# Two subtractions of VectorE issued two steps sooner in the preparation of batch 0's heads

## The chip, the cores and the metric

The kernel runs on one NeuronCore of a Trainium2 chip, in one launch. The metric is the device time of the program in microseconds (us); less is better. Five engines work beside each other and meet at semaphores: TensorE (PE) multiplies into PSUM, VectorE (DVE), ScalarE (ACT) and GpSimd (POOL) do elementwise work, and SyncE (SP) issues DMAs. Each engine takes its own instructions strictly in the order in which they stand in its queue.

## The reference, cut to what matters

```
q, k, v: (2 batches, 8 heads, 768 tokens, 64), proj: (64, 6)
bucket(q), bucket(k) = six sign bits of q @ proj, of k @ proj
scores = q @ k.T / 8, and -1e9 where the buckets differ
x = softmax(scores) @ v
u = x + real(fft over tokens and channels of x)
u = u + relu(layernorm(u) @ w1) @ w2
y = w_tok_r @ (u cos(u @ w_theta)) + w_tok_i @ (u sin(u @ w_theta))
out = (u + y) + relu((u + y) @ w_ch)
```

## The kernel before, in words

All float32 products are done as products of a rounded high part and a low part (the value less its high part): three products, high by high, high by low, and low by high.

Batch 0's attention is the first stage (`attention_first`, L450). It takes the 8 heads as 4 pairs, j = 0 to 3, and for each pair 6 tiles of 128 queries, L = 0 to 5. One tile of one pair, both heads at once, is a step s = 6 j + L; there are 24. In each step TensorE forms the scores of two heads in two of three PSUM tiles (`pair_S`, tile `pss`), VectorE takes the negated maximum of each (TENSOR_REDUCE `nm`), ScalarE takes the two exponentials. Two in three of the exponential tiles are split into high and low by GpSimd (a TENSOR_SCALAR, then a TENSOR_TENSOR) and turned by a DMA. The third is turned by TensorE in two halves (`turn_half`, L364): three transposes into the PSUM tile `psm`, ScalarE's copy of the high part, VectorE's subtraction of the low part. The trace names these tiles by their buffers, p, pt, w1h and w1l, some of them lent from the weights. `psm` has one buffer in this stage, so the second half's transposes wait for the first half's subtraction.

In a step the program gives VectorE, in this order: pieces of the Fourier stage of an older pair (`fold`, tile `fa`), the first halves' subtraction, two maxima, the second halves' subtraction, then the normalisation of a finished pair (r, x) and the preparation of the next pair. Within the stage this order is binding: `Ordered` chains each engine's instructions one behind the other as the program gives them, SP's and GpSimd's DMA issues included. What is outside the stage, the first pair's preparation among it, is ordered by the compiler's list scheduler from priorities and a simulated timeline.

The preparation of pair j + 1 is the generator `prep_pair` (L230), advanced once in a step. Its parts, split by `yield`:

1. At L = 5 of the pair before: the loads of q and k (tile `tt`) on SP.
2. At L = 1: two copies on ScalarE, the high parts `hi` of q and of k (tile `stk`, 0.125 folded into k's).
3. At L = 2: TensorE projects q and k, VectorE makes the sign bits (TENSOR_SCALAR `bits`, from PSUM).
4. At L = 3: TensorE spreads q's bits, ScalarE makes `oh` of q, and VectorE subtracts the low part `lo` of q (SCALAR_TENSOR_TENSOR `stk<-tt,stk`, helper `stt`).
5. At L = 4: the same for k, and the load of v.
6. At L = 3 of the pair's own steps: ScalarE's and VectorE's high and low part of v (`vv`). In a step with L = 3 and j over 0 this stands ahead of part 4 of the next pair.

Both `lo` parts are read by the scores of the next pair, from its L = 0 on.

Of the kernel before, what the change touches and what calls it, by code (L numbers as in the profile page):

```python
# [16 lines left out]
ALU = mybir.AluOpType  # L17
# [16 lines left out]
def f(t):  # L34
    return t.bitcast(F32)
# [35 lines left out]
def fused_kernel(ctx, tc, A, out):  # L71
    nc = tc.nc
    V, AC, PE, PL, SY = (Ordered(tc, e) for e in (nc.vector, nc.scalar, nc.tensor, nc.gpsimd, nc.sync))
# [4 lines left out]
    def mk(p, shape, dt, tag, **kw):  # L78
        return p.tile(shape, dt, tag=tag, name=tag, **kw)

    def mm(o, l, r, st, sp):
        PE.matmul(o, l, r, start=st, stop=sp)
# [4 lines left out]
    def stt(eng, out, in0, in1, op, scale=1.0):  # L87
        if eng is V:
            return V.scalar_tensor_tensor(out=out, in0=in0, scalar=scale, in1=in1, op0=ALU.mult, op1=op)
        assert scale == 1.0  # L90
        return eng.tensor_tensor(out=out, in0=in0, in1=in1, op=op)
# [23 lines left out]
    def PS(k):  # L115
        n = turn[k] % sum(c for _, c in ring[k])
        turn[k] += 1
        for p, c in ring[k]:
            if n < c:
                w = [128, 2, 512] if k == "s" else [128, 512]  # L120
                tag = "psm" if p in [x[0] for x in ring["m"]] else "ps" + k
                return p.tile(w, F32, tag=tag, name=tag)
            n -= c
# [4 lines left out]
    def at(us):  # L128

        tc.cur_priority = int(1000 * us)  # L130
# [99 lines left out]
    def prep_pair(j, first=False):  # L230

        pk = mk(st_p, [128, 4, S], F32R, "stk")
        tt, hi, lo = mk(at_p, [128, 2, S], F32, "tt"), pk[:, 0:2], pk[:, 2:4]
        oh = mk(st_p, [128, 2, S], BF16, "oh")
        for n, k in enumerate(("qT", "kT")):
            if first:
                at(0.2 * n)
            SY.dma_start(out=tt[:, n], in_=A[k][0, j])
        made[j] = [(hi, lo), oh]
        yield  # L240
        for n in range(2):
            gate["start"] = AC.activation(out=hi[:, n], in_=tt[:, n], func=AF.Copy, scale=0.125 if n else 1.0)
        yield
        bits = mk(at_p, [128, 384], BF16, "bits")
        ps = PS("s")[:, 0, 0:384]
        for g in range(2):
            for qk in range(2):
                c = 64 * g + 32 * qk
                mm(ps[c:c + 32], projb, tt[:, qk, 384 * g:384 * g + 384], True, True)
        V.tensor_scalar(out=bits, in0=ps, scalar1=0.0, scalar2=None, op0=ALU.is_gt)  # L250
        yield
        for qk in range(2):
            out = oh[:, qk].rearrange("p (a n) -> p a n", a=2)
            ps = PS("s")
            for g in range(2):
                mm(ps[:, g, 0:384], pat[64 * g:64 * g + 64, 2 + qk], bits[64 * g:64 * g + 64], True, True)
            AC.activation(out=out, in_=ps[:, :, 0:384], func=AF.Sign if qk else AF.Relu, bias=hb[:, qk:qk + 1])
            stt(V, lo[:, qk], tt[:, qk], f(hi[:, qk]), ALU.subtract, 0.125 if qk else 1.0)
            if qk:
                vr = mk(at_p, [128, 2 * NT * (D + 1)], F32, "vr")  # L260
                SY.dma_start(out=vr, in_=A["v"][0, j])
            yield
        v2 = mk(vv_p, [128, 2, 2 * NT * (D + 1)], F16, "vv")
        AC.activation(out=v2[:, 0], in_=vr, func=AF.Copy, scale=VS)
        stt(V, v2[:, 1], vr, v2[:, 0], ALU.subtract, VS)
        made[j].append(v2.rearrange("p a (h k c) -> p a h k c", h=2, k=NT))
# [183 lines left out]
    def attention_first(pace, after):  # L450
# [19 lines left out]
        Ordered.keep = True  # L470
        at(0)
        new = {j: prep_pair(j) for j in range(1, 4)}
        next(new[1])
        for s in range(N + LAG):
# [440 lines left out]
    pick = lambda e, last=None: lambda n: last if last and n >= T["ne"] else e[n % len(e)]  # L915
    at(0.2)
    run(prep_pair(0, True))
    at(T["f0"] - 40)
    with after_gate("start"):
# [249 lines left out]
```

## Time and profile before

| what | value |
|---|---|
| median of 3 runs | 749.19 us (749.02 to 750.71) |
| the profiled execution's own time | 746.12 us |
| its span, first to last instruction | 744.3 us |
| mean granted TensorE clock | 0.943 of full |
| busy: PE, DVE, ACT, POOL | 665.5, 406.1, 381.0, 367.7 us (89%, 55%, 51%, 49%) |
| VectorE in slices 2 to 7 of 40 (18.6 us each) | 5, 6, 8, 7, 8, 7 tenths |

Busy shares are averages over stages with different limits. In the rows below a line begins with the start in us and the time that it took in us; in square brackets stands the time for which the engine had been idle before it, and what ended the idleness.

### The profile page before, as it was taken

The numbers are of one execution on the slowest core, as the hardware profiler recorded it, in microseconds if no ns is written. First come the engines' busy times: TensorE is split into PE (matmuls) and PEld (weight loads), VectorE is DVE, ScalarE is ACT, GpSimd is POOL, SyncE is SP. The second block draws the span as 40 slices with busy tenths as digits, with TensorE's granted clock in tenths as the row PEclk, the third lists the DMA queues.
The fourth block names the chain that finished last, engine by engine and source line by source line (L and its number), as shares of the span: only waits on it lengthen the run. The fifth ranks groups of instructions, "written<-read, shape, count | busy, mean of one in ns | idle before, by whom it ended". The sixth has DMA issues, their size and how long they took to land.

```text
span 744.3 us, 13549 instructions
## 1 busy us (share of the span) xinstructions
PE 665.5 (89%) x5450; PEld 519.8 (70%) x5450; DVE 406.1 (55%) x657; ACT 381.0 (51%) x611; POOL 367.7 (49%) x308
## 2 busy tenths in 40 slices
PE   5897878559677988999999989999999999999997
PEld 2565666448556744787687767488485798999997
DVE  2568787776879853544367592055422266461222
ACT  3564655869798886675413252064425555770010
POOL 2696779588687867877570020023414235850000
PEclk7898989779679998999999999999999999999999
DMA  9896767449989988977851061011004611551202
GB/s 317 193 179 145 129 148 141 97 159 233 200 223 249 241 194 169 178 127 132 135 157 60 6 151 30 1 43 29 1 1 130 209 44 29 170 170 44 85 1 85
DMA packets 161440, 93.70 MB, mean 126 GB/s; under 512 B 137057, under 2 KB 147553, under 8 KB 161377
## 3 DMA queue, kind: packets, MB, share of 16 engines
q1 hardware_dynamic: 159440, 86.27, 50.1%
q0 software_dynamic: 1936, 6.57, 2.6%
q8 instruction: 43, 0.70, 0.4%
q14 instruction: 21, 0.16, 0.1%
HBM read 49.82 MB, written 6.29 MB: 75 GB/s over the span
## 4 chain that ended last, share of the span: by engine, by line
PE 41%; POOL 11%; issue 10%; DMA 7%; ACT 7%; DVE 6%; POOLq 0%; ACTq 0%; DVEq 0%; SPq 0%
PE psm L62 25%; PE psf L62 13%; POOL p L62 3%; POOL w1l L62 2%; ACT r L62 2%; POOL pt L62 2%; DMA r<-in_w 1%; PE pss L62 1%; DMA r<-in_wch 1%; DMA x<-p 1%; PE pso L62 1%; ACT stk L62 1%; DMA r<-in_wtok 1%; DVE fa L62 1%; DVE r L62 1%
## 5 line engine op out<-in xcount | busy, mean ns | idle before, releaser
L62 PE MATMUL psm<-unT,w1h 128*128 128x256 f16 x768 | 130.5, 275 | 5.5 <-DVE u L62 2.9
L62 PE MATMUL psm<-unT,w1l 128*128 128x256 f16 x384 | 105.4, 275 | 0.0
L62 DVE SCALAR_TENSOR_TENSOR r<-r 128x512 uint32<-128x512 uint32 (+1 forms) x64 | 62.8, 986 | 61.0 <-ACT r L62 43.6
L62 PEld LDWEIGHTS <-w1h 128*128 128x128 f16 (+1 forms) x774 | 75.0, 99 | 22.5 <-issue 11.1
L62 PEld LDWEIGHTS <-hh 128*128 128x128 f16 x384 | 37.0, 99 | 43.5 <-issue 2.7
L62 ACT ACTIVATE r<-r,chalf 128x512 uint32<-128x512 uint32 (+1 forms) x64 | 46.1, 721 | 37.2 <-DMA r<-in_wtok 11.7
L62 POOL TENSOR_TENSOR w1l<-r,w1h 128x384 fp32r<-128x384 f32 (+1 forms) x36 | 40.5, 1136 | 47.4 <-ACT w1h L62 47.4
L62 DVE TENSOR_REDUCE nm<-pss 128x1 f32<-128x768 f32 x48 | 45.3, 950 | 31.8 <-PE pss L62 31.7
L62 PE MATMUL psm<-w2h,hh 128*128 128x512 f16 x192 | 61.8, 382 | 0.4 <-DVE hl L62 0.4
L62 PE MATMUL psm<-w2l,hh 128*128 128x512 f16 x192 | 61.5, 383 | 0.0
L62 PE MATMUL psm<-w2h,hl 128*128 128x512 f16 x192 | 61.1, 382 | 0.0
L62 PE MATMUL pss<-stk 128*128 128x384 f32 x192 | 50.1, 391 | 11.7 <-ACT stk L62 6.2
L62 POOL TENSOR_TENSOR p<-p,p 128x768 f16<-128x768 f32 x32 | 54.0, 1691 | 8.1 <-ACT p L62 7.2
L62 DVE SCALAR_TENSOR_TENSOR hl<-psm,hh 128x512 f16<-128x512 f32 x48 | 32.9, 687 | 41.6 <-ACT hh L62 41.3
L62 ACT ACTIVATE p<-pss,nm 128x768 f32<-128x768 f32 x48 | 42.7, 894 | 24.0 <-DVE nm L62 23.9
L62 ACT ACTIVATE hh<-psm 128x512 f16<-128x512 f32 x48 | 28.2, 591 | 50.7 <-PE psm L62 50.6
L64 DVE TENSOR_REDUCE nm<-pss 128x1 f32<-128x768 f32 x48 | 43.6, 949 | 16.0 <-PE pss L64 16.0
L62 PEld LDWEIGHTS pss<-stk 128*128 128x128 f32 x192 | 36.0, 211 | 15.4 <-ACT stk L62 7.6
L62 PEld LDWEIGHTS <-w1l 128*128 128x128 f16 x384 | 37.9, 99 | 6.6 <-issue 2.1
L64 PE MATMUL pss<-stk 64*128 64x384 f32 x288 | 37.3, 382 | 2.6 <-ACT p L64 1.8
L62 ACT ACTIVATE r<-r 128x512 f32<-128x512 f32 (+1 forms) x64 | 39.3, 615 | 0.0
L62 POOL TENSOR_SCALAR nn<-nn 128x512 f32<-128x512 f32 x12 | 7.9, 656 | 61.8 <-ACT nn L62 61.4
(319 smaller groups left out, 1620.9 us busy)
## 6 DMA issues: line engine op xcount, KB each, us to landing
r<-in_w SPq DMA_DIRECT2D x32, 512.0 KB, 4.9
r<-in_wtok SPq DMA_DIRECT2D x24, 384.0 KB, 3.7
vr<-in_v SPq DMA_DIRECT2D x8, 390.0 KB, 3.4
tt<-in_qT SPq DMA_DIRECT2D x8, 384.0 KB, 3.3
tt<-in_kT SPq DMA_DIRECT2D x8, 384.0 KB, 4.1
stk<-stk SPq DMA_DIRECT2D x16, 192.0 KB, 4.2
xT<-xs SPq DMA_DIRECT2D x12, 256.0 KB, 2.6
xt<-xT SPq DMA_DIRECT2D x4, 768.0 KB, 5.7
```

The costliest lines, as they stand in the source:

```text
L62: return fn(*a, **k)
L64: self.last = fn(*a, **k)
```

## The change

The subtraction of q's low part moves from part 4 to part 2, behind ScalarE's two copies; that of k's low part moves from part 5 to part 3, behind the bits. Operands, engine and arithmetic stay.

```diff
         for n in range(2):
             gate["start"] = AC.activation(out=hi[:, n], in_=tt[:, n], func=AF.Copy, scale=0.125 if n else 1.0)
+        stt(V, lo[:, 0], tt[:, 0], f(hi[:, 0]), ALU.subtract)
         yield
         bits = mk(at_p, [128, 384], BF16, "bits")
...
         V.tensor_scalar(out=bits, in0=ps, scalar1=0.0, scalar2=None, op0=ALU.is_gt)
+        stt(V, lo[:, 1], tt[:, 1], f(hi[:, 1]), ALU.subtract, 0.125)
         yield
         for qk in range(2):
...
             AC.activation(out=out, in_=ps[:, :, 0:384], func=AF.Sign if qk else AF.Relu, bias=hb[:, qk:qk + 1])
-            stt(V, lo[:, qk], tt[:, qk], f(hi[:, qk]), ALU.subtract, 0.125 if qk else 1.0)
             if qk:
                 vr = mk(at_p, [128, 2 * NT * (D + 1)], F32, "vr")
                 SY.dma_start(out=vr, in_=A["v"][0, j])
```

## Rows read from the trace of the kernel before

**Rows 1.** Chain of waits, end of batch 0's attention (start us, us, what).
```profile
131.38 1.18 DVE zraw L64
```
**Rows 2.** Timeline of VectorE, first pair's steps (start us, us, engine, line, operation, out<-in).
```profile
9.28 0.96 DVE L62 SCALAR_TENSOR_TENSOR stk<-tt,stk 128x768 fp32r<-128x768 f32 x1 [3.57 <-ACT stk L62]
...
25.82 0.56 DVE L64 TENSOR_TENSOR pt<-psm,pt 128x384 f16<-128x384 f32 x1 [2.81 <-ACT pt L64]
...
28.48 0.55 DVE L64 TENSOR_SCALAR bits<-pss 128x384 bf16<-128x384 f32 x1
30.54 1.82 DVE L64 TENSOR_REDUCE nm<-pss 128x1 f32<-128x768 f32 x2 [1.50 <-PE pss L64]
...
34.58 0.56 DVE L64 TENSOR_TENSOR w1l<-psm,w1l 128x384 f16<-128x384 f32 x1 [1.36 <-ACT w1l L64]
...
39.09 0.56 DVE L64 TENSOR_TENSOR w1l<-psm,w1l 128x384 f16<-128x384 f32 x1 [0.31 <-ACT w1l L64]
```
**Rows 3.** Timeline of VectorE, second pair's steps L = 2 to 5.
```profile
51.42 0.56 DVE L64 TENSOR_TENSOR w1l<-psm,w1l 128x384 f16<-128x384 f32 x1 [2.43 <-ACT w1l L64]
...
54.55 0.56 DVE L64 TENSOR_SCALAR bits<-pss 128x384 bf16<-128x384 f32 x1 [0.38 <-PE pss L64]
56.12 1.82 DVE L64 TENSOR_REDUCE nm<-pss 128x1 f32<-128x768 f32 x2 [1.02 <-PE pss L64]
...
59.73 0.97 DVE L64 SCALAR_TENSOR_TENSOR vv<-vr,vv 128x780 f16<-128x780 f32 x1 [0.90 <-ACT vv L64]
60.62 2.39 DVE L64 SCALAR_TENSOR_TENSOR stk<-tt,stk 128x768 fp32r<-128x768 f32 x1
62.94 1.34 DVE L64 TENSOR_TENSOR fa<-x 128x384 f32<-128x384 f32 x1
64.20 0.55 DVE L64 TENSOR_TENSOR pt<-psm,pt 128x384 f16<-128x384 f32 x1
...
69.51 0.56 DVE L64 TENSOR_TENSOR w1h<-psm,w1h 128x384 f16<-128x384 f32 x1 [0.61 <-ACT w1h L64]
```
**Rows 4.** Timeline of GpSimd, the second pair.
```profile
49.72 1.65 POOL L64 TENSOR_TENSOR p<-w1l,p 128x768 f16<-128x768 f32 x1
51.34 0.83 POOL L64 TENSOR_SCALAR w1h<-p 128x768 f16<-128x768 f32 x1
...
54.90 1.65 POOL L64 TENSOR_TENSOR w1h<-p,w1h 128x768 f16<-128x768 f32 x1
...
59.96 2.24 POOL L64 TENSOR_TENSOR p<-w1l,p 128x768 f16<-128x768 f32 x1
```
**Rows 5.** Timeline of ScalarE, the copies of the third pair's high parts.
```profile
49.44 1.57 ACT L64 ACTIVATE stk<-tt 128x768 fp32r<-128x768 f32 x2
```
**Rows 6.** Timeline of GpSimd and of VectorE, a close meeting in the fourth pair.
```profile
125.11 0.83 POOL L64 TENSOR_SCALAR p<-w1l 128x768 f16<-128x768 f32 x1
...
125.18 1.17 DVE L64 TENSOR_TENSOR fa<-fa 128x384 f32<-128x384 f32 x1
```
**Rows 7.** Timeline of VectorE, the third pair's L = 3.
```profile
91.70 2.39 DVE L64 SCALAR_TENSOR_TENSOR stk<-tt,stk 128x768 fp32r<-128x768 f32 x1
```
**Rows 8.** Timeline of TensorE: pauses, and 36 matmuls with v.
```profile
52.03 0.55 PE L64 MATMUL psm<-ident,pt 128*128 128x128 f32 x3 [0.85 <-DVE w1l L64]
...
64.81 0.90 PE L64 MATMUL psm<-ident,pt 128*128 128x128 f32 x3 [4.14 <-DVE pt L64]
65.50 2.19 PE L64 MATMUL pso<-vv,w1l 128*128 128x65 f16 x36
...
71.08 1.27 PE L64 MATMUL pso<-vv,w1l 128*128 128x65 f16 x36
...
123.05 0.55 PE L64 MATMUL psm<-ident,p 128*128 128x128 f32 x3 [1.89 <-DVE pt L64]
```
**Rows 9.** Windows of 2 us: busy PE, PEld, DVE, ACT, POOL, PE clock, DMA, GB/s.
```profile
66.00:68.00 2.00, 2.00 (x33) 1.63 (x30) 2.00 (x4) 1.82 (x3) 0.89 (x1) 0.50 0.00 0
...
124.00:126.00 2.00, 1.93 (x26) 1.51 (x22) 2.00 (x3) 1.74 (x3) 1.94 (x3) 0.50 0.65 198
```

## The prediction

> **What bounds the kernel now.** I read the chain of waits first, for where the changed stage enters the end. The chain that ended last runs through VectorE at 131.38 us, in the last pieces of batch 0's attention [rows 1], and from there into the conversion of weights and the preparation of batch 1. So I count a microsecond of the stage as a microsecond of the whole, and look only at what the stage gains or loses.
>
> Then the timelines of the stage, engine by engine. A step is a loop: maxima (VectorE), exponentials (ScalarE), the next scores (TensorE, which need a PSUM tile back), the next maxima. No engine is full; whatever stands late in one link moves all later ones. The reader is to see in VectorE's rows what ended each idle time: ScalarE's copy before the first subtraction of a step, TensorE's scores before the maxima [rows 2, 3]. One place differs. At L = 3 of the second pair VectorE works without a gap from 59.73 to 64.20 [rows 3], TensorE stands still for 4.14 us and waits for VectorE's subtraction [rows 8], and in that stretch one of the moved instructions takes 2.39 us, against 0.96 us for the same work alone [rows 2, 3].
>
> **Why 2.39.** The row begins at 60.62 beside a TENSOR_TENSOR of GpSimd that runs from 59.96 to 62.20 [rows 4]. If it works for its usual 0.96 us, it started at 62.05, 0.15 us ahead of the end of GpSimd's row. GpSimd's row in turn is 0.59 us longer than its usual 1.65 [rows 4], which is the rest of the `vv` subtraction. So the two engines take turns: a VectorE instruction with both inputs in SBUF and a GpSimd instruction hold each other off whole, and the one that asked first goes first. At the closest meeting in the stage GpSimd's row begins 0.07 us before VectorE's, and VectorE's takes 1.17 us in place of 0.55 [rows 6]: the earlier one won there too. Subtractions from PSUM and the maxima keep their 0.56 and 0.91 us (1.82 for two) beside GpSimd [rows 3], so they are outside of this.
>
> **The change part by part.** The four preparations are not alike. The first pair's is outside the ordered list, and its two subtractions already run as soon as ScalarE's copies are there, at 9.28 us for k's [rows 2]: nothing moves. Three preparations are left, in the steps of the first, second and third pair.
>
> *Taken away at L = 3.* In the first pair the next subtraction waited 1.36 us for ScalarE [rows 2]: 0 gained. In the second pair the `fa` subtraction comes next. It has two inputs in SBUF, so it waits for GpSimd till 62.05, takes 0.55, and the next one can start at 62.05 + 0.55 - 0.07 (rows on one engine overlap by that much) = 62.53 in place of 64.20 [rows 3, 4]: 1.67 us gained. The third pair has the same row, again 2.39 us [rows 7]: 1.67 more. Together 3.34 us. The bounds of one of them are 0.89 (the instruction's own work, less the overlap) and 2.32 (all of its row); I take the value between because GpSimd's 62.05 stays.
>
> *Taken away at L = 4.* The subtraction behind it waited 0.31 us for ScalarE in the first pair, 0.61 in the second [rows 2, 3], and in the third the step is built the same: 0 gained. SP's loads of the next q and k, which waited for the last reader of `tt`, are issued sooner; their first use is at L = 1, two steps on, and SP's transposes behind them wait for GpSimd's splits: 0, and nothing is lost if they come no sooner.
>
> *Added at L = 1.* q's subtraction waits for ScalarE's first copy, out some 0.8 us after 49.44 [rows 5], at about 50.3. VectorE has nothing to do then (idle for 2.43 us before 51.42 [rows 3]), so by its own length it would fit. But GpSimd's TENSOR_TENSOR has begun at 49.72 and runs to 51.37 [rows 4]. The subtraction starts at 51.37 - 0.15 = 51.22, and what is queued behind it, the first half's subtraction, can start at 51.22 + 0.96 - 0.08 = 52.10 in place of 51.42: 0.68 us lost. TensorE's second transposes wait for that one (0.85 us of pause already [rows 8]), then ScalarE's copy, the exponentials and the next scores: nothing in this loop has slack, so the whole step slides. The bounds are 0 (it slips in ahead of GpSimd, which would need to ask over 0.5 us sooner) and 0.68. GpSimd's next instruction, at 51.34, slides by 0.7 as well. I take 0.68 for each of the three preparations (in the first VectorE's idle time was 2.81 [rows 2]): 2.04 us.
>
> *Added at L = 2.* k's subtraction stands behind the bits. They start at 54.55 and free VectorE after 0.48, at 55.03; with the slide, 55.71. GpSimd's TENSOR_TENSOR begins at 54.90 [rows 4]; with its own slide of 0.70, 55.60. So GpSimd asks 0.11 us sooner, as it won by 0.07 in [rows 6]. Then k's subtraction starts at 55.60 + 1.65 - 0.15 = 57.10, and the maxima behind it at 57.10 + 0.96 - 0.08 = 57.98. They could have started at 56.12 + 0.68 = 56.80: 1.18 us lost. If VectorE asks first, it is done by 56.67 and the 1.02 us of waiting for TensorE [rows 3] covers it: 0. These are the two ends; I take 1.18 in the second and third pair, 2.36 together. In the first pair the maxima had 1.50 us to wait [rows 2], which covers 0.96 of work and half a microsecond of waiting: 0, and 1.1 at most behind a whole TENSOR_TENSOR.
>
> The sum is 2.04 + 2.36 - 3.34 = +1.06 us. Against the profiled execution that makes 746.12 + 1.06 = 747.2; that execution is 3.1 us below the median of the runs, so against the median 749.19 + 1.06 = 750.25. Bound by the other end of the meeting at L = 2 it is -1.30.
>
> The page "SBUF — State Buffer" of the Trainium skill, section "Who interferes with whom", has a rule that speaks against this change: a VectorE instruction with two SBUF inputs and a GpSimd one that reads SBUF block each other for a whole instruction, and the order of issue decides. The trace agrees, by the 2.39 us above. By its whole instruction, without the 0.15 us by which the rows overlap, each of five waits would be 0.15 longer and the `fa` subtraction of both saved places 0.15 later, and the sum 1.06 + 7 x 0.15 = +2.1.
>
> **TensorE's clock.** After the pause of 4.14 us the clock stood at 0.50 of full, 1.2 GHz [rows 8, 9], and 36 matmuls with v took 2.19 us against 1.27 at 2.4 GHz [rows 8]; the three transposes before them took 0.90 against 0.55. That is 0.92 + 0.35 = 1.27 us for one fall of the clock, where TensorE is the late one. My forecast shortens this pause by 1.67 to 2.47 us and still lets the clock fall: after a pause of 1.89 us at 123.05 it fell as well [rows 8, 9].
>
> The page "TensorE: Matmul & The Clock Gate", section "Why this matters for your kernels", says that throughput is held by keeping the pauses between bursts of matmuls short, with a bound that would let 2.47 us pass. By that rule the clock would stay up in both places; the fall after 1.89 us speaks against it.
>
> **The rivals.**
>
> A, the forecast: +1.06, 750.2.
>
> B, VectorE comes first at L = 2 in both pairs: 2.04 - 3.34 = -1.30, 747.9. For it: the lead is only 0.11 us, out of rows whose starts on GpSimd are rough. Against it: [rows 6].
>
> C, the shortened pauses keep the clock at 2.4 GHz: 2 x 1.27 = 2.54 less. With A that is 1.06 - 2.54 = -1.48, 747.7; with B -3.84, 745.4. For it: the pause is cut by two fifths. Against it: the fall at 123.05.
>
> D, on the slower side: the new waits at L = 1 and L = 2 stretch TensorE's pauses and the clock falls where it didn't before. The pause before 52.03 grows from 0.85 to 1.53, and a new one of over a microsecond comes before the scores after L = 2. It decides from somewhere between 0.85, which kept the clock, and 1.89, which lost it. Two falls at 1.27 on top of A: +3.6, 752.8.
>
> E, nothing changes because the stage's end isn't what the rest waits for, or the compiler's list for the later stages, which is made from a simulated timeline, takes up the difference either way: within 0.5 of 749.2. The chain [rows 1] speaks against the first; nothing in the trace can exclude the second.
>
> **How the numbers follow.** A 0.40, B 0.17, C 0.17, D 0.18, E 0.08. The predicted time is A's, 750.2. A by itself, with 0.3 us of doubt in each of its five waits and the later list's order at about 1.5 us either way, is 748.5 to 752. The range takes in B, most of C and D: 746.0 to 753.0. A measurement of this kernel tells about 0.3%, 2.2 us, from no change: faster is below 746.9, slower above 751.4. Faster has half of C, some of B: 0.16. Slower has D and an edge of A: 0.22. The same has the rest: 0.62.
>
> **What would show it.** At L = 1 the row of q's subtraction is about 1.9 us long, begins at a time when GpSimd's TENSOR_TENSOR runs, and the subtraction behind it no longer waits for ScalarE. At L = 2 of the second and third pair k's row is over 2 us under A, 0.96 under B. At L = 3 the stretch from `vv` to the first subtraction shrinks from 4.47 us to 2.8. TensorE's clock after that pause, and between the bits and the scores, tells C and D. The prediction is wrong if q's subtraction at L = 1 takes 0.96 us, if the step behind it doesn't slide, or if the stage ends over 2 us sooner or later than in the sum while its rows are as said.

## The result, and the profile after

The changed kernel takes 743.3 us (median of 5 runs, 741.98 to 746.14) against 749.19 (5 runs, 748.82 to 750.71): a ratio of 0.992, with a 95% interval of 0.9898 to 0.9942. It is faster by some 6 us, where the prediction said 750.2 and its range began at 746.0. The profiled execution took 743.55 us with a span of 741.8 and a mean granted clock of 0.939. That is only 2.6 us less than the profiled execution of before (746.12), which lies 3 us under its median: the traces below tell where time went, the medians how much.

Inside the changed stage the forecast held. VectorE's timeline of the second pair, L = 1 to 3, after the change (start us, us, engine, line, operation, out<-in; in brackets the idle time before and what ended it):

```profile
53.02 1.89 DVE L64 SCALAR_TENSOR_TENSOR stk<-tt,stk 128x768 fp32r<-128x768 f32 x1 [1.32 <-ACT stk L64]
54.83 0.55 DVE L64 TENSOR_TENSOR w1l<-psm,w1l 128x384 f16<-128x384 f32 x1
55.29 1.81 DVE L64 TENSOR_REDUCE nm<-pss 128x1 f32<-128x768 f32 x2
...
57.94 0.56 DVE L64 TENSOR_SCALAR bits<-pss 128x384 bf16<-128x384 f32 x1 [0.37 <-PE pss L64]
58.41 2.35 DVE L64 SCALAR_TENSOR_TENSOR stk<-tt,stk 128x768 fp32r<-128x768 f32 x1
60.68 1.81 DVE L64 TENSOR_REDUCE nm<-pss 128x1 f32<-128x768 f32 x2
...
64.28 0.97 DVE L64 SCALAR_TENSOR_TENSOR vv<-vr,vv 128x780 f16<-128x780 f32 x1 [0.90 <-ACT vv L64]
65.17 1.99 DVE L64 TENSOR_TENSOR fa<-x 128x384 f32<-128x384 f32 x1
67.08 0.55 DVE L64 TENSOR_TENSOR pt<-psm,pt 128x384 f16<-128x384 f32 x1
```

In the kernel before, the maxima that precede those of 56.12 [rows 3] stand here:

```profile
51.89 1.81 DVE L64 TENSOR_REDUCE nm<-pss 128x1 f32<-128x768 f32 x2
```

GpSimd's TENSOR_TENSORs that three of the rows after the change meet (q's and k's `stk`, and `fa`):

```profile
52.43 1.66 POOL L64 TENSOR_TENSOR p<-w1l,p 128x768 f16<-128x768 f32 x1
...
58.29 1.64 POOL L64 TENSOR_TENSOR w1h<-p,w1h 128x768 f16<-128x768 f32 x1
...
64.50 2.24 POOL L64 TENSOR_TENSOR p<-w1l,p 128x768 f16<-128x768 f32 x1
```

TensorE's pauses in these steps:

```profile
55.43 0.55 PE L64 MATMUL psm<-ident,pt 128*128 128x128 f32 x3 [1.51 <-DVE w1l L64]
...
62.69 0.48 PE L64 MATMUL pss<-oh 64*128 64x384 bf16 x2 [0.91 <-ACT w1h L64]
63.56 1.32 PE L64 MATMUL pss<-stk 64*128 64x384 f32 x12 [0.39 <-ACT w1l L64]
...
67.68 0.75 PE L64 MATMUL psm<-ident,pt 128*128 128x128 f32 x3 [2.47 <-DVE pt L64]
68.22 2.19 PE L64 MATMUL pso<-vv,w1l 128*128 128x65 f16 x36
```

The reader is to see that each row of [rows 3, 8] went where the sum put it. q's subtraction waits behind GpSimd and takes 1.89 us; TensorE's pause behind it is 1.51 (forecast 1.53, before 0.85). k's asks at 58.41, 0.12 behind GpSimd's 58.29, loses the meeting and takes 2.35; from the maxima before it to those behind it are 60.68 - 55.29 = 5.39 us, in place of 56.12 - 51.89 = 4.23. At L = 3 the time from `vv` to the first subtraction is 67.08 - 64.28 = 2.80 (forecast 2.8, before 4.47), and TensorE's pause is 2.47 in place of 4.14. The third pair repeats it with 1.89 and 2.35.

So the gain isn't in this stage. It shows later, in TensorE's windows (length, busy PE, PEld, DVE, ACT, POOL with the number of instructions, PE clock, DMA share, GB/s). Before:

```profile
260.00:300.00 40.00, 33.03 (x256) 19.05 (x255) 19.82 (x23) 27.33 (x38) 27.40 (x21) 0.91 0.85 192
...
440.00:445.00 5.00, 2.45 (x23) 2.19 (x23) 5.00 (x11) 4.34 (x8) 0.00 (x0) 1.00 1.05 185
```

And after:

```profile
260.00:300.00 40.00, 37.03 (x312) 22.86 (x312) 23.56 (x28) 32.04 (x45) 32.02 (x23) 1.00 0.97 224
...
440.00:445.00 5.00, 5.00 (x49) 4.47 (x47) 5.00 (x12) 4.75 (x9) 0.54 (x1) 1.00 0.63 225
```

From 455 us on TensorE is full for a long stretch in both (25.0 us of the 25 to 480). What it stood idle ahead of that can't be made up there; before the change TensorE worked 4.0 us less in the first window and 2.55 less in the second. The two waits that stand out there, in TensorE's timeline of the kernel before:

```profile
285.82 1.17 PE L62 MATMUL pso<-vv,pt 128*128 128x65 f16 x18 [3.66 <-DMA pt<-pt]
...
439.02 0.60 PE L62 MATMUL psf<-ident,u 128*128 128x128 f32 x4
442.55 0.38 PE L62 MATMUL psm<-unT,w1h 128*128 128x256 f16 x2 [2.93 <-DVE u L62]
```

No instruction of these stages is changed. What differs is their order. Up to the end of the stage the issue orders of the two compiled programs are alike on every engine, but for the six moved instructions and for two loads on SyncE: those of batch 1's first q and k stand three places sooner (issued at 91.64 and 92.02 us, before the change at 98.91 and 99.29). Behind it the compiler's list scheduler has put other instructions at 1614 of TensorE's 5418 places, at 199 of VectorE's 649 and 172 of ScalarE's 609, up to about 450 us. From here on "old list" and "new list" are the orders of the later stages in the kernel before and in the changed one; these two loads go with the list.

### The profile page after: what moved, and what is told of

It reads as the page before. It is cut to its first block, busy times and chain, and to the rows that moved or that the text cites. A ratio compares the mean times of both kernels' runs of the same rounds, so it can differ in the third digit from the quotient of the medians.

```text
span 741.8 us, 13545 instructions
## 1 busy us (share of the span) xinstructions
PE 672.3 (91%) x5450; PEld 525.9 (71%) x5450; DVE 407.4 (55%) x657; ACT 380.2 (51%) x611; POOL 370.1 (50%) x308
## 4 chain that ended last, share of the span: by engine, by line
PE 41%; issue 7%; POOL 7%; DMA 6%; ACT 4%; DVE 3%; SPq 0%; POOLq 0%; ACTq 0%; DVEq 0%
PE psm L62 25%; PE psf L62 14%; POOL p L62 2%; DMA pt<-pt 2%; POOL pt L62 1%; DMA x<-p 1%; DMA pt<-p 1%; PE pss L62 1%; DVE fa L62 1%; ACT p L62 1%; ACT r L62 1%; POOL w1l L62 1%; POOL stk L62 1%; PE pso L62 1%; DMA r<-in_wch 1%
## 5 line engine op out<-in xcount | busy, mean ns | idle before, releaser
L62 DVE SCALAR_TENSOR_TENSOR r<-r 128x512 uint32<-128x512 uint32 (+1 forms) x64 | 60.6, 957 | 54.9 <-ACT r L62 47.3
L62 PE MATMUL psm<-w2h,hh 128*128 128x512 f16 x192 | 60.1, 379 | 0.1
L62 PE MATMUL psm<-w2l,hh 128*128 128x512 f16 x192 | 59.6, 379 | 0.0
L62 POOL TENSOR_TENSOR stk<-tt,stk 64x768 fp32r<-64x768 f32 x16 | 31.3, 1954 | 11.1 <-issue 7.9
```

Source lines behind the costliest of these rows:

```text
L62: return fn(*a, **k)
```

## The experiments

**Stage and list apart.** Theory L: the new list made the gain, the stage a small loss. Rivals: the stage is worth more than its rows say, because it hands over to the later stages better (S), or only both together gain (I). Each engine's instructions are chained in a written order by edges that only fix the order (no semaphore, no wait); the arithmetic stays. No run times the kernel before chained in its own order, so that the chaining itself costs nothing rests on the product of ratios below.

```diff
+def pin_order(tc):
+    """Every engine's instructions in the order listed, by NoSync edges."""
...
+    for e, order in issue_orders().items():
+        for a, b in zip(order, order[1:]):
+            tc.add_manual_dep(by[e][b], by[e][a].name, edge, reason="pin_order")
...
         fused_kernel(tc, aps, out)
+        pin_order(tc)
```

The changed stage with the old list:

> All five engines' orders are written out as those of the kernel before, but for the six moved subtractions, which stand where the changed kernel has them. So it has the changed stage and the old list for everything behind it. Theory L (the compiler's list for the later stages made the gain; the stage itself lost 1.06 us by the sum, 3.0 in the one trace of the changed kernel, of which some 2 are TensorE's clock falling in the first pair): 750.2 to 752.2 us, ratio 1.001 to 1.004. Rival S (the later work went sooner because the stage hands over differently, whatever the list): about 743.3, ratio 0.992. Rival I (a list only fits the stage it was made for): slower than 752.

Measured: 1.0026 [1.0001, 1.0051], that is +2 us (0.1 to 3.8). The stage of before with the new list:

> The converse: the orders of the changed kernel on all engines, with the six subtractions back where the kernel before has them. Theory L: the whole gain of the list without the stage's loss, 743.3 less 1 to 3, so 740.3 to 742.3 us, ratio 0.988 to 0.991. Rival S: 749.2, ratio 1.000. Rival I: between, 743 to 749.

Measured: 0.9902 [0.9865, 0.9939], -7.3 us. The product is 0.9928; the change itself, compiled without a written order, is 0.992, so neither the chaining nor a joint effect of stage and list is needed to explain it. Both ratios lie in the ranges of L, and S is out. I is less likely by the points, but the intervals reach into its ranges (slower than 752, and 743 to 749). The change's gain is the list's, and the version without the change but with the new list is as fast as the changed kernel.

**The two moves apart, both with the old list.** In the first only q's subtraction is moved, in the second only k's:

```diff
+        stt(V, lo[:, 0], tt[:, 0], f(hi[:, 0]), ALU.subtract)          # q only
...
+        stt(V, lo[:, 1], tt[:, 1], f(hi[:, 1]), ALU.subtract, 0.125)   # k only
```

> Old list for everything; of the six, q's three stand at L = 1, k's three stay at L = 4. By the sum for the stage: 3 x 0.68 - 2 x 1.67 = -1.30 us, so 747.9; in the trace q's rows at L = 1 take 1.9 us and the step behind slides by 0.68, and L = 3 gives back 1.67 in the second and third pair. If the collisions with GpSimd aren't the price, q's rows are 0.96 and the gain is 3.3. TensorE's clock may add or take 1 to 3.

Measured: 0.9987 [0.9957, 1.0017], -1.0 us.

> Old list for everything; k's three stand at L = 2 behind the bits, q's three stay at L = 3. By the sum: nothing gained at L = 4, 1.17 us lost in the second and third pair where GpSimd comes first by 0.13 us, so +2.3, 751.5; k's rows there are about 2.3 us. If the meeting goes to VectorE, rows of 0.96 and no change, 749.2.

Measured: 1.0038 [1.0008, 1.0067], +2.8 us. Both stand where the rows put them, though q's interval holds no change too. In the trace of the first q's rows at L = 1 are 1.82, 1.88 and 1.89 long, in that of the second k's rows at L = 2 of the second and third pair 2.35. q's move is the useful half by the rows, k's the harmful one.

**Where the list gains.** The new list up to matmul 3300 of TensorE, some 387 us, and the old one behind it; and the converse. The stage is that of before.

> The stage as before the change; behind it the new list up to matmul 3300 of TensorE (about 387 us) and the old list from there. Theory M: the gain is made in the middle, where TensorE was busy for 37.0 us of the 40 from 260 us on with the new list and for 33.0 with the old; the whole gain of some 7 us comes with this part: ratio 0.990 to 0.994 to the kernel before. Theory E: the gain is made at the end of this part of the work, at 440 to 446 us, where TensorE has run out of matmuls with the old list and waits for the last tiles of u (2.5 us of 5 idle) and with the new one has not; a lead won in the middle is only waited away there: 0.998 to 1.002. Theory M+E, half from each: 0.994 to 0.997.

Measured: 1.0007 [0.9976, 1.0037].

> The converse: the stage as before the change, the old list up to matmul 3300 of TensorE and the new one from there. Theory M: 0.998 to 1.002. Theory E: 0.990 to 0.994, and no idle time of TensorE between 440 and 446 us. Theory M+E: 0.994 to 0.997.

Measured: 0.9952 [0.9926, 0.9977]. The first run has the fuller middle and no gain. Neither trace is of a typical execution: the first run's took 747.15 us, the shortest of its 12 (median 751.19), the second's 750.58, the longest of its 12 (median 746.52). So they show which pauses stand, not what they cost. The first run's windows:

```profile
260.00:300.00 40.00, 38.80 (x338) 24.75 (x338) 22.39 (x31) 32.95 (x46) 32.49 (x23) 1.00 0.97 208
...
440.00:445.00 5.00, 2.09 (x17) 1.59 (x16) 5.00 (x13) 3.73 (x8) 0.24 (x1) 1.00 0.88 220
```

And its pauses behind 385 us, in TensorE's timeline:

```profile
391.53 0.59 PE L62 MATMUL psm<-unT,w1h 128*128 128x256 f16 x2 [2.71 <-DVE hl L62]
...
443.96 0.38 PE L62 MATMUL psm<-unT,w1h 128*128 128x256 f16 x2 [2.91 <-DVE u L62]
```

The second is that of the old end. The first stands right behind the seam of the two lists; the traces of the old and of the new list by themselves show no pause of TensorE from 385 to 420 us, so the lead of the middle is waited away in part at a pause that only this mixture has. The second run has the old middle and the new end:

```profile
260.00:300.00 40.00, 32.10 (x226) 18.45 (x225) 21.77 (x21) 29.76 (x44) 27.34 (x21) 0.91 0.84 190
...
440.00:445.00 5.00, 5.00 (x35) 3.23 (x34) 4.83 (x26) 2.79 (x6) 2.96 (x3) 1.00 0.13 20
```

It gains 3.6 us, half of the new list's 7.3. M is out by both runs, M+E by the first. E is the one left whose ranges both intervals touch, but its 0.990 to 0.994 was missed by the point. The two parts multiply to 0.9959, and the whole list gave 0.9902; the difference of 0.0057 is barely more than the noise of the three ratios taken together (0.0054). That the middle counts only where the end doesn't wait would fit this. It isn't shown, for the pause at the seam spoils the run that would tell.

**The wait at the end by itself.** In VectorE's timeline of the kernel before, the additions `u<-psm,u`, which empty the PSUM tiles that TensorE wants, stand behind four normalisations, of which the first two take 3.03 us:

```profile
436.07 3.03 DVE L62 TENSOR_SCALAR x<-u,mv,rs 128x512 f32<-128x512 f32 x2
...
440.44 0.99 DVE L62 TENSOR_SCALAR x<-u,mv,rs 128x512 f32<-128x512 f32 x2
...
441.82 1.27 DVE L62 SCALAR_TENSOR_TENSOR u<-psm,u 128x512 f32<-128x512 f32 x2
```

After the change the same additions come ahead of them:

```profile
436.13 0.69 DVE L62 SCALAR_TENSOR_TENSOR u<-psm,u 128x512 f32<-128x512 f32 x1 [0.17 <-PE psm L62]
...
436.81 0.68 DVE L62 SCALAR_TENSOR_TENSOR u<-psm,u 128x512 f32<-128x512 f32 x1
...
439.23 2.06 DVE L62 TENSOR_SCALAR x<-u,mv,rs 128x512 f32<-128x512 f32 x2
```

Two kernels, the kernel before and the one with the new list up to 390 us, get just this in the written order of VectorE (four short instructions between are left out):

```diff
 x<-u,mv,rs  x2
+u<-psm,u    x2
 u<-x,u
 u<-x,u
 x<-u,mv,rs  x2
-u<-psm,u    x2
```

> The kernel before in its own order, with one thing moved: on VectorE the last two additions u<-psm,u, which stand behind the four normalisations x<-u,mv,rs and free the PSUM tiles for which TensorE waits 2.93 us at 442.55, go ahead of the last two of these. If that wait is on the path by itself (part of theory E), TensorE's pause shrinks from 2.93 to about 0.5 us and the whole by 2.4: ratio 0.997. Rival: the pause is only handed on, TensorE waits as long for the next tiles of u, whose low parts come 1.2 us later: 0.999 to 1.002.

Measured: 0.9972 [0.9948, 0.9996], -2.1 us.

> The same move of the two additions in the kernel that has the new list up to 390 us and the old one behind (1.0007). If the old end is only bad by this wait, the lead of the middle comes through and the ratio is near that of the whole new list: 0.990 to 0.993. If the wait is worth its own 2.4 us and no more: 0.9975. If it is handed on: 1.000 to 1.002.

Measured: 0.9988 [0.9965, 1.001]. TensorE's timeline of the first:

```profile
438.95 0.60 PE L62 MATMUL psf<-ident,u 128*128 128x128 f32 x4
439.69 0.38 PE L62 MATMUL psm<-unT,w1h 128*128 128x256 f16 x2
...
449.83 0.38 PE L62 MATMUL psm<-unT,w1h 128*128 128x256 f16 x2 [2.12 <-DVE hl L62]
```

The pause of 2.93 us is gone, so it was VectorE's order that made it. But another of 2.12 us, for VectorE's `hl`, comes 10 us later. The time fell by 2.1 us (0.3 to 3.9), as by the theory that the wait is on the path; the trace shows most of the pause handed on, as by its rival, whose 0.999 lies within the interval, and the two profiled executions took the same time (746.11 and 746.12). How much of the pause was on the path stays open. In the second kernel the new pause is 1.96 us, the 2.72 behind the seam stays, and the lead of the middle doesn't come through: the expectation of 0.990 to 0.993 fell; 0.9975 lies within the interval, and 1.000, the pause handed on, does too.

**How often does the list turn?** Three kernels go without a written order, with part of the change each; one more, told first, keeps the new list and tries what the rows call the best stage. Their edits are the diff of the change, in part, and a condition on the pair:

```diff
+        if j >= 2:    # q_two_pairs_list_new; j == 2: third pair; j == 3: fourth; none: q only
+            stt(V, lo[:, 0], tt[:, 0], f(hi[:, 0]), ALU.subtract)
```

> Only q's subtraction is moved, and only in the preparations of the third and fourth pair, where the place at L = 3 gives 1.67 us back and the place at L = 1 costs 0.68; k's and the other pairs' stay where they were before the change. Behind the stage the new list is kept. By the rows of the stage the sum is 2 x 0.68 - 2 x 1.67 = -2.0 us, on top of the ratio of 0.990 that the new list gave with the old stage: 0.9876, about 740 us where the kernel before takes 749.2. Rival: what the stage gains is waited away later in a fixed order, and the ratio stays at 0.990.

Measured: 741.29 us, 0.9877 [0.9841, 0.9913], against 0.9876 expected. It is the version that the experiments pointed to: its ratio is below that of both kernels, and its interval lies apart from no change, but not from the changed kernel's 0.9898 to 0.9942. It holds the rival's 0.990 too, so what the better stage adds isn't shown, and a hit to the fourth digit is luck.

> q's subtractions moved in all preparations, k's not, and the later stages in the order that the compiler's list scheduler makes for this program by itself. The stage alone gave 0.9987 with the old list. Theory L (the later order is chance, and worth up to 1%): a ratio that the stage does not foretell, anywhere from 0.985 to 1.005, and more than 0.003 away from 0.9987 in about two cases of three. Rival: the new list was a gain of this one program, others stay with the old one's time: 0.996 to 1.001.

Measured: 741.91 us, 0.9877 [0.9835, 0.9919]; the rival's 0.996 to 1.001 is out. "Anywhere" was too wide, though: the order that the compiler made is the new list, but for 5 places of SyncE, those about the two loads named above, and 0.9902 x 0.9987 = 0.989 would have foretold it. So the loads aren't the gain either. For k's move alone the compiler makes the old list, place by place.

> One instruction of the kernel before is moved: q's subtraction in the preparation of the third pair. By the rows of the stage it gains 1.67 - 0.68 = 1.0 us, a ratio of 0.9987. The compiler makes a third order of the later stages for it, which differs from the old one at 1684 of TensorE's 5418 places and from the new one at 1312. Theory L: the later order sets most of the time, and whether TensorE stands idle between 260 and 300 us and between 440 and 446 us tells which way: with both pauses 0.997 to 1.001, with one 0.992 to 0.997, with none 0.986 to 0.991. Rival: only the stage counts, 0.9987 whatever the pauses.

Measured: 0.9925 [0.99, 0.9949]. Its trace has neither of the two pauses, though shorter ones of 1.57 and 2.09 us stand between 260 and 270 us:

```profile
260.00:300.00 40.00, 37.09 (x316) 22.28 (x317) 23.25 (x25) 31.34 (x46) 33.26 (x24) 0.96 1.01 231
...
440.00:445.00 5.00, 5.00 (x48) 4.49 (x46) 4.60 (x23) 2.56 (x5) 3.39 (x3) 1.00 0.80 235
```

By that the expectation was 0.986 to 0.991: the direction was right, the size missed. The two windows don't tell all of a list's worth. The rival's 0.9987 is out.

> One instruction of the kernel before is moved: q's subtraction in the preparation of the fourth pair, again 1.0 us by the rows of the stage. The order that the compiler makes for the later stages differs from the new list at 54 of TensorE's 5418 places only, from the old one at 1643. Theory L: 0.990 of the new list x 0.9987 = 0.989, and no pause of TensorE at 440 to 446 us. Rival: only the stage counts, 0.9987.

Measured: 741.6 us, 0.9885 [0.9845, 0.9925], where 0.989 was expected. One moved instruction is worth over 8 us here (5.6 to 11.7), of which its own stage, by the sum of its rows, accounts for 1.

## Why the prediction was wrong

**The step that failed** is the assumption that opens it, "I count a microsecond of the stage as a microsecond of the whole, and look only at what the stage gains or loses", with its guard, rival E: "the compiler's list for the later stages, which is made from a simulated timeline, takes up the difference either way: within 0.5 of 749.2", at 0.08, and the later list's order at "about 1.5 us either way". The mechanism was named; its size and its direction were not. It is -7.3 us (0.9902 [0.9865, 0.9939]), five times the doubt given to it, and it doesn't absorb the stage's difference but adds to it. What the runs put in place of the step: the list by itself is worth the whole gain, the changed stage by itself costs about 2 us. The profile before showed where such a term could come from: pauses of 3.66 and 2.93 us on an engine that is full afterwards. I read only the chain up to 131 us and the stage's own rows.

**The sum of the stage** was +1.06; the changed stage with the old list measured +2 us (0.1 to 3.8). Its terms:

- *L = 1, 0.68 lost in each preparation:* rows of 1.89, and TensorE's pause longer by 0.66. In the first pair q's row was 1.26 long (1.82 to 1.93 in three other kernels with q moved there) and TensorE's clock differed, so 0.68 can't be read there.
- *L = 2, 1.18 lost:* k's row 2.35, and the distance between the maxima on either side longer by 1.16 (5.39 against 4.23). Rival B (0.96) is out: k's row was 2.34 or 2.35 in both pairs of all three kernels with k moved. k alone cost 2.8 us (0.6 to 5.0).
- *L = 3, 1.67 gained:* 4.47 - 2.80 = 1.67, in both pairs. q alone gave 1.0 us net, where 2.04 - 3.34 = -1.30 was expected.
- *Turns:* k's subtraction ended at 58.41 + 2.35 = 60.76; if it ran its own 0.96 us, it began at 59.80, 0.13 before the end of GpSimd's row. The page "SBUF — State Buffer" of the Trainium skill, section "Who interferes with whom", has a whole instruction wait for the other; the trace agrees but for this 0.13 us.

**TensorE's clock.** In the changed kernel it fell behind the pause of 2.47 us to 0.50 of full, 1.2 GHz, from 68 to 70 us, and 36 matmuls took 2.19 us, as forecast: no saving as in rival C. Behind the lengthened pauses of 1.51, 0.91 and 0.39 us it held, so rival D doesn't come in the second and third pair of this kernel. But D isn't dead. With k's move alone TensorE's pauses ahead of the scores are nearly the same (0.94 and 0.38 us), and in the second pair the clock fell there (0.50 from 63 us on):

```profile
62.34 1.94 PE L64 MATMUL pss<-stk 64*128 64x384 f32 x12 [0.38 <-ACT w1l L64]
```

These matmuls took 1.33 us in the third pair of that kernel and 1.32 in the changed kernel's second, at full clock. So the length of a pause, by which D was to be decided, doesn't tell by itself: 1.51 us kept the clock here, 0.94 and 0.38 lost it once. In the first pair the clock tells little of D: its mean from 20 to 40 us was 0.59 in both traces with both subtractions moved there, and anything from 0.50 to 1.00 in the nine with none moved there. With k left in its place, the pauses ahead of the scores don't come, and the fall behind the shortened pause is later (TensorE in the kernel with q moved in two pairs):

```profile
66.23 0.55 PE L64 MATMUL psm<-ident,pt 128*128 128x128 f32 x3 [2.45 <-DVE pt L64]
66.61 1.78 PE L64 MATMUL pso<-vv,w1l 128*128 128x65 f16 x36
...
96.39 0.55 PE L64 MATMUL psm<-ident,w1l 128*128 128x128 f32 x3 [2.48 <-DVE w1l L64]
96.78 1.34 PE L64 MATMUL pso<-vv,pt 128*128 128x65 f16 x36
```

The clock fell all the same, to 0.50 from 68 to 70 us and from 98 to 100, but in one pair only part of the 36 matmuls came under it (1.78 us) and in the other hardly any (1.34). Part of what rival C counted on is gained there.

**A reading to be wary of.** The stage ended at 131.38 us before and at 134.42 after, 3.0 us later, and only 1.1 of it is in the rows above. In three other kernels with the stage of before it ended at 132.50, 135.13 and 135.22, with the granted clock from 20 to 40 us at 0.76, 0.61 and 0.74 (0.87 in the trace before, 0.59 after). One trace can't tell such a microsecond, nor give it to the clock of the first pair, as the expectation for the changed stage with the old list did; pairs of rows inside the stage can.

What stays open is why the scheduler turns to the new list for q's move in the later pairs and not for k's or q's in the second, and what else in a list costs time beside the two windows. It also stays open how the gain divides between the middle and the end.

## What to carry to other kernels

Where a compiler orders later stages from a simulated timeline, an edit ahead of them is two changes: its own, and another order of everything behind it. Forecast the first from the rows, give the second a term of its own (here up to 1% of the time for one moved instruction), and measure them apart with the order written out; else a harmful move is kept for a gain that isn't its own. Pauses of the engine that is full at the end, wherever they stand, tell how much an order could give; closing one counts only if the next wait doesn't take it up.

## What was not expected of the hardware

Two like pairs of VectorE's TENSOR_SCALARs, `x<-u,mv,rs`, took 3.03 us at 436.07 and 0.99 at 440.44 in the trace before. GpSimd's timeline there:

```profile
433.58 5.25 POOL L62 TENSOR_TENSOR wthl<-r,wthh 128x512 fp32r<-128x512 f32 x4 [34.64 <-ACT wthh L62]
```

It works until 438.83 and then stands still. In the changed kernel GpSimd's four instructions end at 440.54, 1.3 us after the first such pair has begun, and that pair takes 2.06 us; the second, alone, again 0.99. The instruction has one tensor from SBUF as its input, so by these lengths the turns aren't kept to instructions with two, as the prediction had it. The page "SBUF — State Buffer" of the Trainium skill, section "Who interferes with whom", counts a tensor_scalar in a two-port mode among those that can take turns with GpSimd; the lengths fit that, though no run shows that this one ran in such a mode, and none took GpSimd's work away. In the old list the pair of 3.03 us stands ahead of the additions that free TensorE's PSUM tiles, so a part of the 2.93 us probably comes from this meeting.
